# Loads, the V scratch and the opening of a fused attention and feed-forward kernel, rearranged

## The chip, the cores and the metric

The kernel runs on one core of a Trainium2 chip. The metric is the time of one execution on the device in microseconds (us), as the median of several runs. The engines are named as in the profile: PE (TensorE, matrix products), PEld (its loads of the stationary operand), DVE (VectorE), ACT (ScalarE), POOL (GpSimd) and SP (SyncE, which here only issues DMA transfers).

## The reference, cut to what matters

One transformer block is computed on 2048 tokens of width 512, in bfloat16. A modulation vector made from `c` and `w_mod` gives six rows of 512: shift, scale and gate of the attention (`sa`, `ca`, `ga`) and of the feed-forward part (`sb`, `cb`, `gb`).

```python
mod = (silu(c) @ w_mod).reshape(1, 6, 1, 512)
sa, ca, ga, sb, cb, gb = (mod[:, i] for i in range(6))
h = layernorm(x) * (1 + ca) + sa
q, k, v = split(h @ wqkv)                  # 32 heads of 16
idx = pos[:, None] - 2 * arange(8)         # each token sees 8 keys, 0, 2, .. 14 back
logits = einsum('hsd,hswd->hsw', q, k[idx]) * 16 ** -0.5   # -1e9 where idx < 0
x = x + ga * (einsum('hsw,hswd->hsd', softmax(logits), v[idx]) @ wo)
h = layernorm(x) * (1 + cb) + sb
x = x + gb * ((gelu(h @ w_gate) * (h @ w_up)) @ w_down)    # inner width 1792
```

## The kernel before

The tokens are worked on in four groups of 512, numbered 0 to 3 (`sg`). For each group the steps are these.

- `ln1`: mean and variance on DVE (L404, L405), the inverse root on POOL (L413), the normalized rows `xn` on DVE (L419).
- `t1`: the rows are transposed to `hT`. Group 0 does it on PE (L432) and scales while it leaves PSUM (L460 on DVE, L463 on ACT); the other groups use a transposing DMA issued by SP (L439) and scale in place on ACT (L447).
- `qkv`: twelve products of four matmuls each (L491), in the order q0, k0, v0 to v3, q1, k1, q2, k2, q3, k3; ACT copies each from PSUM (L506 q, L508 k, L512 v).
- `vload`: V of the group is stored to a scratch `vscr` in device memory (L518) and read back four times (L527), one read for each of four shifts, each into 32 of the 128 partitions of the tile `V`, so that the partitions hold V at the distances 0, 2, 4 and 6.
- `logits`, `soft`, `pv`: products of q and shifted k on DVE (L541), summed over the head on PE (L555), softmax, probabilities transposed on PE (L640), products with `V` on DVE (L658), summed on PE (L670).
- `x1`: product with `wo` (L690), added to x on DVE (L699); then `ln2`, another transposing DMA (`h` from `xn`, L439) and scaling on ACT (L447).
- `ffn`: 14 pairs of products with `w_gate` and `w_up` (L718), gelu and copy on ACT (L742, L749), their product on DVE (L760), 8 half products with `w_down` (L731), the residual on DVE (L767), and the store.

The program text doesn't fix the order of these steps. Each step is an `Op` of a thread; the threads have priorities from the table `PR` (lower goes first), one value for each kind of step and group. `Planner.run` takes the step that can begin first by its own model of engine times (`w`), buffers (`take`, `give`) and events (`after`, `fire`); among the steps of that engine that can begin within a tolerance (`slack`, or `far` for steps whose priority is better by 8 or more) it takes the one with the best priority. That order is then the program of each engine, and each engine executes its program strictly in order.

All loads but three are issued by SP, in the order of `sp_q`: x of group 0 in four pieces, the q and k blocks of `wqkv`, x of group 1, the v block of `wqkv`, x of groups 2 and 3, block 2 of `w_mod` (the row `ga`), four pieces of `wo`, blocks 3 and 4 of `w_mod` (for `mod1`, the second layer norm), block 5 (the row `gb`, by which `w_down` is scaled), then `w_gate` and `w_up` once V of group 0 has been read back, and `w_down` at the end. ACT issues `c` and the blocks 1 and 0 of `w_mod`, which the first layer norm needs (`mod0`). Until the first product PE runs 16 matmuls on zeros (`warmup`, L248).

`wqkv` lies in one tile `[128, DT, 3 * D]`: the three blocks are side by side inside each of the four slices `dt` over which a product sums. The scratch `vscr` is one tensor over all groups with rows of 2048 + 16.

## Time and profile before

| what | us |
|---|---|
| median of 3 runs | 254.66 (254.41 to 255.35) |
| profiled execution, its own time | 255.11 |
| its span, first to last instruction | 253.2 |
| PE busy / DVE busy / ACT busy / POOL busy | 240.3 / 185.2 / 144.6 / 15.3 |
| first product of `qkv` starts (L491) | 13.27 |
| first product of `ffn` of group 0 starts (L718) | 78.47 |
| last product ends | 249.7 |

The profile covers one execution. A busy PE is not PE at its peak: a single matmul of 128x512 shows 379 ns, but a row of them is started every 216 ns (56 matmuls of L731 take 12.10 us), and with the clock granted at one half every 0.43 us. `x8` in the timeline means eight instructions merged into one row, and the text in brackets is the time the engine had been idle before and what ended it. In the chain of waits a DMA row is the time from issue to landing.

### The profile page before, as it was taken

The page shows a single profiled execution, that of the slowest core. Times are in us where ns is not written, and L with a number is a line of the kernel's source. Part 1 is how long each engine was busy: PE and PEld are TensorE (multiplying, and loading weights), DVE is VectorE, ACT ScalarE, POOL GpSimd, SP SyncE. Part 2 cuts the span into 40 slices and gives each one's busy share as a digit, 9 for nine tenths or more (in the row PEclk, how much of TensorE's full clock was granted, in tenths as well). Part 3 has the DMA queues.
Part 4 walks back from the last instruction along what each step waited for, and adds up shares of the span by engine and source line. Part 5 has one row for each costly group of instructions (what it writes and reads, how often), then busy time and mean ns, then how long its engine had stood idle before and what let it go on. Part 6 is the DMA issues. An engine that isn't in the chain of part 4 may idle for free.

```text
span 253.2 us, 3608 instructions
## 1 busy us (share of the span) xinstructions
PE 240.3 (95%) x1353; PEld 105.2 (42%) x1353; DVE 185.2 (73%) x295; ACT 144.6 (57%) x237; POOL 15.3 (6%) x37
## 2 busy tenths in 40 slices
PE   6789698899999999999999999999999999999994
PEld 2444334434443433444444334444344444444441
DVE  3499949999999999999999969688948422222221
ACT  2065459978569967430796763448654730766400
POOL 3410003000200000002000001000001000000000
PEclk9799979999999999999999999999999999999999
DMA  6999899999983500973300069510000401000011
GB/s 213 350 332 283 166 193 188 356 346 255 198 190 116 183 0 0 203 137 71 81 16 1 0 129 197 116 43 23 0 0 3 84 21 52 11 4 0 0 41 41
DMA packets 37417, 29.41 MB, mean 116 GB/s; under 512 B 15512, under 2 KB 36248, under 8 KB 37400
## 3 DMA queue, kind: packets, MB, share of 16 engines
q1 hardware_dynamic: 36336, 28.14, 47.2%
q10 hardware_dynamic: 1064, 1.05, 1.3%
q8 instruction: 10, 0.16, 0.3%
q14 instruction: 7, 0.06, 0.1%
HBM read 21.32 MB, written 4.19 MB: 101 GB/s over the span
## 4 chain that ended last, share of the span: by engine, by line
PE 71%; DMA 14%; DVE 7%; ACT 5%; SPq 1%; issue 1%; DVEq 0%; ACTq 0%
PE y_ps L731 19%; PE g_ps L718 19%; PE u_ps L718 19%; DMA wm<-in_w_mod_dram 5%; PE x_ps L690 5%; PE qkv_ps L491 4%; PE o_ps L670 3%; DMA x<-in_A_x_dram 3%; DMA hT<-xn 3%; DMA h<-xn 2%; DVE st L404 2%; DVE pq L541 2%; ACT hT L447 1%; PE LTp L555 1%; ACT h L447 1%; DVE xn L419 1%
## 5 line engine op out<-in xcount | busy, mean ns | idle before, releaser
L718 PE MATMUL g_ps<-h,Wg 128*128 128x512 bf16 x224 | 57.9, 379 | 0.6 <-ACT h L447 0.3
L718 PE MATMUL u_ps<-h,Wu 128*128 128x512 bf16 x224 | 57.6, 379 | 0.0
L491 PE MATMUL qkv_ps<-hT,wqkv 128*128 128x512 bf16 x192 | 47.3, 390 | 3.9 <-ACT hT L447 2.6
L731 PE MATMUL y_ps<-WdP,hht 128*128 128x512 bf16 x224 | 49.3, 379 | 0.0
L742 ACT ACTIVATE gl<-g_ps 128x512 bf16<-128x512 f32 x56 | 33.5, 599 | 26.7 <-PE g_ps L718 23.3
L749 ACT CAST ub<-u_ps 128x512 bf16<-128x512 f32 x56 | 33.0, 588 | 20.2 <-PE u_ps L718 20.2
L760 DVE TENSOR_TENSOR hht<-gl,ub 128x512 bf16<-128x512 bf16 x56 | 23.5, 420 | 28.1 <-ACT ub L749 27.5
L658 DVE TENSOR_TENSOR pv<-PT,V 128x2048 bf16<-128x2048 bf16 x32 | 37.8, 1219 | 1.0 <-ACT PT L646 1.0
L541 DVE TENSOR_TENSOR pq<-qT,kT 128x2048 bf16<-128x2048 bf16 x32 | 37.8, 1216 | 0.4 <-ACT kT L508 0.4
L718 PEld LDWEIGHTS <-Wg 128*128 128x128 bf16 x224 | 21.1, 98 | 28.5 <-issue 4.6
L731 PEld LDWEIGHTS <-hht 128*128 128x128 bf16 x224 | 21.8, 98 | 26.4 <-issue 0.4
L718 PEld LDWEIGHTS <-Wu 128*128 128x128 bf16 x224 | 21.1, 98 | 27.7 <-issue 4.0
L491 PEld LDWEIGHTS <-wqkv 128*128 128x128 bf16 x192 | 20.9, 115 | 26.5 <-issue 9.8
L404 DVE BATCH_NORM_STATS2 st<-x 128x6 f32<-128x512 bf16 x32 | 21.7, 680 | 6.4 <-DMA x<-in_A_x_dram 6.3
L767 DVE TENSOR_TENSOR ot<-y_ps,x 128x512 bf16<-128x512 f32 x16 | 11.0, 687 | 21.1 <-PE y_ps L731 21.1
L413 POOL TENSOR_TENSOR rstd<-rstd,neghalf 128x4 f32<-128x4 f32 x8 | 10.7, 1340 | 178.9 <-DVE rstd L409 178.9
L447 ACT ACTIVATE h<-h,modT,scl 128x512 bf16<-128x512 bf16 x16 | 11.7, 803 | 7.1 <-DMA h<-xn 7.0
L690 PE MATMUL x_ps<-woP,oT 128*128 128x512 bf16 x64 | 15.6, 379 | 0.0
L508 ACT CAST kT<-qkv_ps 128x512 bf16<-128x512 f32 x16 | 9.2, 586 | 5.8 <-PE qkv_ps L491 5.8
L419 DVE TENSOR_SCALAR xn<-x,mv,rstd 128x512 bf16<-128x512 bf16 x32 | 11.4, 408 | 1.6 <-POOL rstd L413 1.5
L512 ACT CAST vT<-qkv_ps 128x512 bf16<-128x512 f32 x16 | 9.4, 588 | 5.2 <-PE qkv_ps L491 5.1
L699 DVE TENSOR_TENSOR x<-x_ps,x 128x512 bf16<-128x512 f32 x16 | 10.8, 683 | 1.7 <-PE x_ps L690 1.5
(62 smaller groups left out, 157.7 us busy)
## 6 DMA issues: line engine op xcount, KB each, us to landing
V<-vscr SPq DMA_DIRECT2D x12, 520.0 KB, 9.7
wm<-in_w_mod_dram SPq DMA_DIRECT2D x4, 512.0 KB, 9.8
vscr<-vT SPq DMA_DIRECT2D x4, 512.0 KB, 7.1
out_dram<-ot SPq DMA_DIRECT2D x16, 128.0 KB, 1.7
Wg<-in_B_w_gate_dram SPq DMA_DIRECT2D x1, 1792.0 KB, 7.5
Wu<-in_B_w_up_dram SPq DMA_DIRECT2D x1, 1792.0 KB, 11.9
WdP<-in_B_w_down_dram SPq DMA_DIRECT2D x1, 1792.0 KB, 7.5
wqkv<-in_A_wqkv_dram SPq DMA_DIRECT2D x3, 512.0 KB, 7.4
```

The costliest lines, as they stand in the source:

```text
L404: nc.vector.bn_stats(out=st_k["st"][:, c4, :], in_=src()[:, c4, :])
L419: nc.vector.tensor_scalar(out=B[key][:, c4, :], in0=src()[:, c4, :], scalar1=st_k["mv"][:, c4, 0:1], scalar2=st_k["rstd"][:, c4:c4 + 1], o ...
L447: nc.scalar.activation(out=h, in_=h, func=ACT.Identity, scale=sc(dt), bias=bi(dt))
L491: nc.tensor.matmul(ps[:].rearrange("p (c k) -> p c k", k=P), lhsT=wqkv[:, dt, blk * D + j:(blk + 1) * D:4], rhs=B["hT", sg][:, :, dt, :], ...
L541: nc.vector.tensor_tensor(out=pq[:], in0=_ap(B["qT", sg][:, j, :], [[0, 4], [1, SG]]), in1=_ap(kT[:, j, k0:k0 + SG], [[2, 4], [1, SG]]), o ...
L658: nc.vector.tensor_tensor(out=t[:], in0=_ap(B["PT", sg][:, wg, :], [[0, 4], [1, SG]]), in1=B["V4", sg][:, :, j, c0:c0 + SG], op=ALU.mult)
L690: nc.tensor.matmul(ps[:], lhsT=B["oT", sg][:, j, c4 * P:(c4 + 1) * P], rhs=woP[:, j, :], start=(j == 0), stop=(j == 3))
L718: nc.tensor.matmul(ps[:].rearrange("p (c k) -> p c k", k=P), lhsT=Wt[:, dt, ft * P:(ft + 1) * P], rhs=B["h2T", sg][:, :, dt, :], start=(dt ...
L731: nc.tensor.matmul(ps[:], lhsT=B["hh", sg, ft][:, c4 * P:(c4 + 1) * P], rhs=B["WdP"][:, ft, :], start=(ft == 0), stop=(ft == FT - 1))
L742: nc.scalar.activation(out=gl[:], in_=B["g", sg, ft][:], func=ACT.Gelu_apprx_tanh)
L749: nc.scalar.copy(out=ub[:], in_=B["u", sg, ft][:])
L760: nc.vector.tensor_tensor(out=hh[:], in0=B["gl", sg, ft][:], in1=B["ub", sg, ft][:], op=ALU.mult)
```

## The change

- `wqkv` becomes a tile `[128, 3, DT, D]`, each block on its own.
- The loads are cut into threads. `q_head` issues, all from SP: x of group 0 in two pieces (128 and 384 rows), blocks 1 and 0 of `w_mod`, q and k blocks, x of group 1, v block, x of group 2. Block 2 of `w_mod`, `wo` and x of group 3 may be issued only after the transposing DMA of group 1 has been; blocks 3, 4, 5, `w_gate` and `w_up` only after the reads of V of group 0 have been issued (and `w_gate` after the transposing DMA of group 2).
- The scratch is one tensor per group with rows of 512 + 16. The 16 positions before a group (the halo) are written into the tile `vT` by POOL (zeros for group 0, a copy of the end of the group before for the others). Each of the four reads takes, for each of 32 partitions, one contiguous run of 16 rows of 528, shifted by 0, 2, 4 or 6 elements, with `max_dma_last_dim=4 * VL`. The memsets of `V` on POOL go.
- The opening: the zeros for the warm-up come from DVE; the inverse root of group 0 is computed for rows 0 to 255 and 256 to 511 separately; the transposes of group 0 run in two halves; ACT reads one of the two PSUM tiles and DVE the other (before, both read both); `hT` of group 0 is contiguous; three further warm-up matmuls may run after `mod0`'s products.
- The planner's model gets eight DMA lanes, a hold of SP by the transposing DMA, an event "issued" (`!`) beside "landed", and other tolerances; the table `PR` is new.

```diff
@@ -16,15 +16,15 @@
 NEG = -1.0e9
 
 PR = {
-    "ga": 28, "mb": 30.4, "gb": -2.8, "wds": 56.8, "wos": 73.9, "ln1": [33.1, 16.9, 32.7, 29.1], "t1": [-35.2,
-    55, 3.9, 6.5], "h1": [4.7, 2.3, 4.2, 1], "qkv": [15, 5.4, 30.8, 36], "qev": [40, 53.9, 9, 22.7], "v":
-    [14.4, 70, 13, 46.1], "pq": [7.4, 84.3, 109.8, 154.6], "lmm": [4.5, 21.5, -2.4, 5.1], "lev": [2.2, 19.8,
-    38.5, 5.6], "smm": [4.6, 25, 3, -0.9], "soft": [23, 19.5, 1.7, 8.3], "e": [64, 19.2, 103, 16], "ptp": [8,
-    7.1, -1.7, 4.8], "pt": [-10.8, 0.2, 10.5, 42.3], "pv": [2.4, 11.1, 71.1, 29.2], "pvmm": [35.5, 31.3, 3.8,
-    4.1], "pvev": [-14.5, 64.7, 32.1, 40], "x1mm": [18.6, 1.6, -24.2, -9.1], "x1": [-12.8, 1.5, -0.7, -2],
-    "ln2": [28.5, 36.7, 1.4, 68.5], "t2": [1.8, -14.8, 3.9, 0.1], "h2": [-1, 17.3, -2, 10.1], "ffn": [45.9,
-    18, 20.7, 56.2], "act": [30.1, -13.5, -2.2, 57.1], "hh": [-5.2, -5.3, 0, 14.6], "st": [150.1, 14.3, 34.2,
-    31.2],
+    "q_wo": 19, "q_x": 40.9, "q_mb": -18, "q_gu": 55.1, "q_gb": -2.9, "vh": [44.4, 26.2, 17.2, 8], "ga": 87.3,
+    "mb": 20.6, "gb": 46.7, "wds": 31.8, "wos": 60.7, "ln1": [-10.7, 9, 24.7, 45.5], "t1": [-5.1, 14, 28,
+    19.5], "h1": [75.6, 67.7, -7.2, 8.7], "qkv": [13, 45.1, 43.6, 18], "qev": [95.8, 82.9, 35.4, 21.7], "v":
+    [70.1, 13.2, 40, 68.2], "pq": [42.8, 53, 75, 125], "lmm": [41.9, 0.2, 23, 40], "lev": [-14.8, 25.2, 8.6,
+    3], "smm": [-5.5, 13.4, 4.2, 31.5], "soft": [-9.7, 67.5, -8.6, 16.8], "e": [1.6, 53, 28, 33], "ptp":
+    [18.1, 0.5, 23, 4.1], "pt": [69.4, -1.3, 75.9, 32.8], "pv": [3, 6.6, 70, 44.8], "pvmm": [-9.7, 48, 33.5,
+    2], "pvev": [4, 48.8, 13.4, -0.6], "x1mm": [-2.1, 23.9, -6.5, -5.8], "x1": [-11.9, -1.2, -1.9, 23], "ln2":
+    [6, 56.2, 1.4, 23.4], "t2": [11.4, 40, 125.6, 7.2], "h2": [-6.5, -7.1, -11.7, 3], "ffn": [73.6, 51.6,
+    22.1, 81.7], "act": [40, -0.2, 18, 21.3], "hh": [-49, -19.9, -2.8, 7.2], "st": [1.4, 3.2, 13.1, 32.5],
 }
...
-        self.slack = {"PE": 0.51, "ACT": 0.68, "DVE": 0.14, "POOL": 0, "SP": 0}
-        self.far = {"PE": 0, "ACT": 0.05, "DVE": 0.21, "POOL": 0, "SP": 0}
+        self.slack = {"PE": 0.63, "ACT": 0.21, "DVE": 20.96, "POOL": 0, "SP": 84.59}
+        self.far = {"PE": 0, "ACT": 0.22, "DVE": 0.2, "POOL": 0, "SP": 10.66}
         self.table = None
         self.quad = False
         self.dma = 0.0
+        self.lanes = [0.0] * 8
...
             if op.dma:
                 self.dma = max(self.dma, t) + (op.lat or 0.0)
-                fin = max(end, self.dma) + self.LAT["SP"]
+                if op.hold:
+                    end = self.clock[eng] = max(end, self.dma)
+                fin = max(end if not op.hold else 0.0, self.dma) + self.LAT["SP"]
+                self.lanes = self.lanes[1:] + [fin]
             else:
                 fin = end + self.LAT[eng]
             for s in op.give:
                 s.free.append(fin)
             if op.fire:
                 self.done[op.fire] = fin
+                self.done[op.fire + "!"] = end
...
-    vscr = dram.tile([P, 4, VR], BF16, name="vscr")
+    vscr = [dram.tile([P, 4, VL], BF16, name=f"vscr{g}") for g in range(NSG)]
...
-    wqkv = pools["wA"].tile([P, DT, 3 * D], BF16, name="wqkv", tag="wA")
+    wqkv = pools["wA"].tile([P, 3, DT, D], BF16, name="wqkv", tag="wA")
...
-            B["V4", 0] = T("v4", [P, 4, 4, SG + 8], BF16, "V4")
-            for w4 in range(4):
-                nc.gpsimd.memset(B["V4", 0][H * w4:H * w4 + H, :, :, 0:8 + 2 * w4].rearrange("p i j s -> p (i j) s"), 0.0)
-        yield Op("POOL", 3.0, f2, take=[SL["v4"]], fire="M2", after=["LN1.0.rs"])
-
-    def warmup():
-        for k in range(16):
+        yield Op("POOL", 1.9, f2, fire="M2", after=["LN1.0.rs2"])
+
+    def warmup(n, zero):
+        if zero:
+            yield Op("DVE", 0.25, lambda: nc.vector.memset(gB[:], 0.0), fire="warm")
+        for k in range(n):
             def f(k=k):
                 if k == 0:
                     B["warm"] = T("mm", [P, SG], F32, "warm_ps")
-                nc.tensor.matmul(B["warm"][:], lhsT=ident[:], rhs=gB[:], start=True, stop=True)
-            yield Op("PE", 0.43, f, after=["warm"], take=[SL["mm"]] if k == 0 else [],
-                     give=[SL["mm"]] if k == 15 else [])
-
+                nc.tensor.matmul(B["warm"][:], lhsT=gB[:, 0:P], rhs=gB[:], start=True, stop=True)
+            yield Op("PE", 0.43, f, after=["warm"] if zero else ["warm", "mp0"], take=[SL["mm"]] if k == 0 else [],
+                     give=[SL["mm"]] if k == n - 1 else [])
+
+    ORDER = (0, 1, 2, 3)
...
-                (nc.scalar if b < 2 else nc.sync).dma_start(
+                nc.sync.dma_start(
...
-            return ld(wqkv[:, :, b * D:(b + 1) * D], wq_v[:, :, b * D:(b + 1) * D])
+            return ld(wqkv[:, b, :, :], wq_v[:, :, b * D:(b + 1) * D])
...
-            yield Op("ACT", 0.55, ldwm(1), take=[SL[WM[1]]], fire="wm1", lat=mb(0.5), dma=True)
-            yield Op("ACT", 0.55, ldwm(0), take=[SL[WM[0]]], fire="wm0", lat=mb(0.5), dma=True)
-
-        def sp_q():
-            for k in range(CPS):
-                yield Op("SP", 0.5, ldx(0, k, k + 1), fire=f"x0.{k}", lat=mb(0.125))
-            yield Op("SP", 0.55, ldq(0), fire="wqkv0", lat=mb(0.5))
-            yield Op("SP", 0.55, ldq(1), fire="wqkv1", lat=mb(0.5))
-            yield Op("SP", 0.55, ldx(1), fire="x1", lat=mb(0.5))
-            yield Op("SP", 0.55, ldq(2), fire="wqkv2", lat=mb(0.5))
-            yield Op("SP", 0.55, ldx(2), fire="x2", lat=mb(0.5))
-            yield Op("SP", 0.55, ldx(3), fire="x3", lat=mb(0.5))
-            yield Op("SP", 0.55, ldwm(2), take=[SL[WM[2]]], fire="wm2", lat=mb(0.5))
+
+        def q_head():
+            yield Op("SP", 0.45, ldx(0, 0, 1), fire="x0.0", lat=mb(0.125))
+            yield Op("SP", 0.45, ldx(0, 1, 4), fire="x0.1", lat=mb(0.375))
+            yield Op("SP", 0.5, ldwm(1), take=[SL[WM[1]]], fire="wm1", lat=mb(0.5))
+            yield Op("SP", 0.5, ldwm(0), take=[SL[WM[0]]], fire="wm0", lat=mb(0.5))
+            yield Op("SP", 0.5, ldq(0), fire="wqkv0", lat=mb(0.5))
+            yield Op("SP", 0.5, ldq(1), fire="wqkv1", lat=mb(0.5))
+            yield Op("SP", 0.5, ldx(1), fire="x1", lat=mb(0.5))
+            yield Op("SP", 0.5, ldq(2), fire="wqkv2", lat=mb(0.5))
+            yield Op("SP", 0.5, ldx(ORDER[2]), fire=f"x{ORDER[2]}", lat=mb(0.5))
+
+        def q_wo():
+            yield Op("SP", 0.5, ldwm(2), take=[SL[WM[2]]], fire="wm2", lat=mb(0.5), after=["LN1.1.t!"])
             for i in range(4):
-                yield Op("SP", 0.55, ld(woP[H * i:H * i + H, :, :], wo_v[i]), fire=f"wo{i}", lat=mb(0.125))
-            yield Op("SP", 0.65, ldwm(3), take=[SL[WM[3]]], fire="wm3", lat=mb(0.5))
+                yield Op("SP", 0.5, ld(woP[H * i:H * i + H, :, :], wo_v[i]), fire=f"wo{i}", lat=mb(0.125))
+
+        def q_x():
+            yield Op("SP", 0.5, ldx(ORDER[3]), fire=f"x{ORDER[3]}", lat=mb(0.5), after=["LN1.1.t!"])
+
+        def q_mb():
+            yield Op("SP", 0.65, ldwm(3), take=[SL[WM[3]]], fire="wm3", lat=mb(0.5), after=["V4ld.0!"])
             yield Op("SP", 0.65, ldwm(4), take=[SL[WM[4]]], fire="wm4", lat=mb(0.5))
-            yield Op("SP", 0.65, ldwm(5), take=[SL[WM[5]]], fire="wm5", lat=mb(0.5))
-            yield Op("SP", 0.65, ld(Wg[:], wg_v), fire="Wg", lat=mb(1.8), after=["V4ld.0"])
+
+        def q_gu():
+            yield Op("SP", 0.65, ld(Wg[:], wg_v), fire="Wg", lat=mb(1.8), after=["V4ld.0!", f"LN1.{ORDER[2]}.t!"])
             yield Op("SP", 0.65, ld(Wu[:], wu_v), fire="Wu", lat=mb(1.8))
+
+        def q_gb():
+            yield Op("SP", 0.65, ldwm(5), take=[SL[WM[5]]], fire="wm5", lat=mb(0.5), after=["V4ld.0!", "wm2!"])
+
+        def q_d():
             yield Op("SP", 0.65, ldwd, fire="Wd", lat=mb(1.8), take=[SL["wA"]], after=[f"qkv.{g}.l" for g in range(NSG)])
...
-        yield Op("SP", 2.3, f, after=[f"{ev}.x3"], take=[SL[dtag]], give=[SL["xn"]], fire=f"{ev}.t", lat=2.0)
+        yield Op("SP", 1.8, f, after=[f"{ev}.x3"], take=[SL[dtag]], give=[SL["xn"]], fire=f"{ev}.t", lat=1.9, hold=True)
...
+        for dd in range(2):
+            for dtp in range(2):
                 dt = 2 * dtp + dd
 
                 def f(dt=dt, dtp=dtp, dd=dd):
                     if dt == 0:
-                        B[dkey] = T(dtag, [P, CPS, DT, P], BF16, dtag)
-                    hp, h = B[key, dtp][:, dd, :].rearrange("p (c k) -> p c k", k=P), B[dkey][:, :, dt, :]
-                    if dve_share and dd == 1:
-                        nc.vector.tensor_scalar(out=h, in0=hp, scalar1=sc(dt), scalar2=bi(dt),
-                                                op0=ALU.mult, op1=ALU.add)
+                        B[dkey] = T(dtag, [P, DT, SG], BF16, dtag)
+                    hp, h = B[key, dtp][:, dd, :], B[dkey][:, dt, :]
+                    if dtp:
+                        nc.vector.tensor_scalar(out=h, in0=hp, scalar1=sc(dt), scalar2=bi(dt), op0=ALU.mult, op1=ALU.add)
                     else:
-                        nc.scalar.activation(out=h, in_=hp, func=ACT.Identity,
-                                             scale=sc(dt), bias=bi(dt))
-                onv = dve_share and dd == 1
-                yield Op("DVE" if onv else "ACT", 0.54 if onv else 0.68, f, after=[f"{ev}.t{dtp}"] + dep,
+                        nc.scalar.activation(out=h, in_=hp, func=ACT.Identity, scale=sc(dt), bias=bi(dt))
+                yield Op("DVE" if dtp else "ACT", 0.61 if dtp else 0.70, f, after=[f"{ev}.t{dtp}"] + dep,
                          take=[SL[dtag]] if dt == 0 else [], give=[SL["tp"]] if dd == 1 else [], fire=f"{ev}.h{dt}")
...
+        yield from norm(("xn1", sg), lambda: B["x", sg], lambda c4: [f"x0.{min(c4, 1)}"] if sg == 0 else [f"x{sg}"], ev,
+                        ((0, 2), (2, 4)) if sg == 0 else ((0, 4),))
+        pl.done[ev] = pl.done[f"{ev}.x3"]
...
+                        B["vT", sg] = T("vs", [P, 4, VL], BF16, "vT")
+                    nc.scalar.copy(out=B["vT", sg][:, j, VH:VL], in_=ps[:])
             yield Op("ACT", 0.53, g, after=[f"qp.{sg}.{blk}.{j}"], give=[SL["mm"]], fire=f"qkv.{sg}.{blk}.{j}")
...
+    def vhalo(sg):
+        def f():
+            if sg == 0:
+                nc.gpsimd.memset(B["vT", 0][:, :, 0:VH], 0.0)
+            else:
+                nc.gpsimd.tensor_copy(out=B["vT", sg][:, :, 0:VH], in_=B["vT", sg - 1][:, :, SG:VL])
+        yield Op("POOL", 0.4, f, after=[f"qkv.{sg}.2.3"] + ([f"vst.{sg - 1}"] if sg else []), give=[SL["vs"]] if sg else [],
+                 fire=f"vh.{sg}")
+
     def vload(sg):
         def f():
-            nc.sync.dma_start(out=vscr[:, :, VH + sg * SG:VH + (sg + 1) * SG], in_=B["vT", sg][:])
-        yield Op("SP", 0.65, f, after=[f"qkv.{sg}.2.3"], give=[SL["vs"]], fire=f"vst.{sg}", lat=1.5)
+            nc.sync.dma_start(out=vscr[sg][:], in_=B["vT", sg][:])
+        yield Op("SP", 0.65, f, after=[f"vh.{sg}"], give=[SL["vs"]] if sg == NSG - 1 else [], fire=f"vst.{sg}", lat=1.5)
         for w4 in range(4):
             def f(w4=w4):
-                if w4 == 0 and sg:
-                    B["V4", sg] = T("v4", [P, 4, 4, SG + 8], BF16, "V4")
-                z = 0 if sg else 8 + 2 * w4
-                src = bass.AP(vscr.tensor, vscr.offset + VH + sg * SG - 8 - 2 * w4 + z,
-                              [[16 * VR, H], [VR, 16], [1, SG + 8 - z]])
-                nc.sync.dma_start(
-                    out=B["V4", sg][H * w4:H * w4 + H, :, :, z:SG + 8].rearrange("p i j s -> p (i j) s"), in_=src)
-            yield Op("SP", 0.65, f, after=[f"vst.{sg}", "M2"], take=[SL["v4"]] if w4 == 0 and sg else [],
-                     fire=f"V4.{sg}.{w4}" if w4 < 3 else f"V4ld.{sg}", lat=2.8)
+                if w4 == 0:
+                    B["V4", sg] = T("v4", [P, 4 * 4, VL], BF16, "V4")
+                t, n = B["V4", sg], 4 * 4 * VL
+                d = t[H * w4:H * w4 + H, :, :].rearrange("p r s -> p (r s)")
+                src = bass.AP(vscr[sg].tensor, vscr[sg].offset, [[n, H], [1, n - 2 * w4]])
+                nc.sync.dma_start(out=d[:, 2 * w4:n], in_=src, max_dma_last_dim=4 * VL)
+            yield Op("SP", 0.65, f, after=[f"vst.{sg}"], take=[SL["v4"]] if w4 == 0 else [],
+                     fire=f"V4.{sg}.{w4}" if w4 < 3 else f"V4ld.{sg}", lat=1.7)
...
-                    c0 = 8 - 8 * wg
+                    c0 = VH - 8 * wg
                     nc.vector.tensor_tensor(out=t[:], in0=_ap(B["PT", sg][:, wg, :], [[0, 4], [1, SG]]),
-                                            in1=B["V4", sg][:, :, j, c0:c0 + SG], op=ALU.mult)
+                                            in1=B["V4", sg][:, j:16:4, c0:c0 + SG], op=ALU.mult)
...
+    pl.spawn(0.2, mods())
+    pl.spawn(0.5, warmup(16, True))
+    pl.spawn(30, warmup(3, False))
```

## Prediction

> **What bounds the kernel now.** I read first the page's 40 slices (6.33 us each), for the engine that sets the end.
>
> ```profile
> PE   6789698899999999999999999999999999999994
> DVE  3499949999999999999999969688948422222221
> PEclk9799979999999999999999999999999999999999
> DMA  6999899999983500973300069510000401000011
> ```
>
> From about 84 us on PE is full and at full clock to the end: what the change saves there it can only save by starting earlier. The gaps lie in the first 84 us, where DMA is full too (11 slices) and DVE nearly. So I asked the timeline of PE for that stretch.
>
> ```profile
> 13.27 0.38 PE L491 MATMUL qkv_ps<-hT,wqkv 128*128 128x512 bf16 x1 [0.48 <-ACT hT L463]
> 14.19 5.99 PE L491 MATMUL qkv_ps<-hT,wqkv 128*128 128x512 bf16 x27 [0.54 <-DMA wqkv<-in_A_wqkv_dram]
> ...
> 27.55 0.61 PE L555 MATMUL LTp<-pq,Mph 128*32 128x512 bf16 x8
> 29.82 0.38 PE L491 MATMUL qkv_ps<-hT,wqkv 128*128 128x512 bf16 x1 [1.66 <-ACT hT L447]
> ...
> 32.24 0.72 PE L555 MATMUL LTp<-pq,Mph 128*32 128x512 bf16 x8
> 32.90 3.44 PE L491 MATMUL qkv_ps<-hT,wqkv 128*128 128x512 bf16 x8
> ...
> 43.54 1.04 PE L338 MATMUL mb_ps<-wm,scT 128*128 128x512 bf16 x4 [0.72 <-DMA wm<-in_w_mod_dram]
> ```
>
> The second matmul of all waits for `wqkv`; the first product of group 1 waits for `hT`, and then eight matmuls take 3.3 us instead of 1.7. The granted clock by stretch (columns: length, then PE, PEld, DVE, ACT, POOL busy, clock, DMA share, GB/s) says why:
>
> ```profile
> 28.00:32.00 4.00, 1.36 (x8) 0.45 (x4) 3.90 (x8) 3.04 (x5) 0.94 (x1) 1.00 0.95 188
> 32.00:36.00 4.00, 4.00 (x17) 1.31 (x17) 1.39 (x5) 2.53 (x7) 0.07 (x1) 0.58 1.12 196
> ```
>
> PE was busy for 1.36 of 4 us, and in the next 4 us it got 0.58 of its clock. What made `hT` late is in the chain of waits (start, length):
>
> ```profile
> 4.18 8.37 DMA x<-in_A_x_dram
> ...
> 17.92 2.35 DVE pq L541 x2
> 20.26 1.29 DVE xn L419 x4
> 21.59 7.35 DMA hT<-xn
> 28.96 0.82 ACT hT L447
> 29.88 13.61 DMA wm<-in_w_mod_dram
> ```
>
> Two products `pq` stand before the normalized rows on DVE; the transposing DMA takes 7.35 us, where the three undisturbed ones for `h` take 4.3, because `wo` and three blocks of `w_mod` are queued ahead of it; block 5 of `w_mod` lands 13.6 us after its issue, behind the reads of V.
>
> **A ledger of PE** from 13.27 to 249.72, 236.45 us. Work at full clock: 936 matmuls of 128x512 at 0.216 = 202.2; 256 quarter-array ones at 0.55 per eight = 17.6; 64 transposes at 0.45 per eight = 3.6; 32 of `modT` 0.9; 32 changes back from quarter arrays at 0.11 (0.97 against 0.86 for four matmuls) = 3.5. Together 227.8, so 8.7 are lost: 0.7 at 13.27; 4.7 between 27.55 and 36.17 (8.62 less two eights, twelve matmuls and two changes); 0.7 at 43.5; 0.6 before `PTp` at 46.9; 1.1 where `ffn` of group 0 begins (78.47 to 83.64); 0.9 in crumbs. The change can win these 8.7 at most and what comes off the 13.27 before them.
>
> **Part by part.**
>
> *Opening.* x of group 0 and blocks 1 and 0 of `w_mod` are the same 1.6 MB that landed by 8.4; now x goes first. Its first piece landed at 3.0; the other 0.39 MB at 348 GB/s (the mean of 8 to 18 us) take 1.1 more, so some 5.1 instead of 7.8. Then: statistics of the second row block (0.69 + 0.18) and addition 0.17 to 6.2, POOL 1.0; meanwhile two more statistics to 7.9, addition to 8.1, POOL to 9.1, two `xn` at 0.35 to 9.9, eight transposes 0.7 to 10.7, ACT 0.77 twice: slice 0 at 11.6, slice 1 at 12.4; DVE's two (0.54) end before. `mod0` comes at 9.3 as before and is not last. So products start at 11.7. The wait for `wqkv` at 14.19 is a false one: the q block had landed at 9.55, but the second slice of q lies inside the span of the v block's write in the common tile, and that load landed at 14.1 (6.17 + 7.9). With separate blocks the q and k products (eight matmuls) run before v lands; v itself lands no earlier, since the same 3.7 MB are ahead of it. At 14.2 eight matmuls are done instead of one: 7 x 0.216 = **-1.5**. Bounds: -2.5 (PE as early as `hT`, with v early) to +0.8 (one queue starts slower than two: up to 4 us both moved little, 55 to 274 GB/s by half microseconds).
>
> *Group 1.* With priority 9 against 42.8 the normalization now precedes `pq`: x at 12.6, four statistics 3.5, addition and POOL 1.4, four `xn` 1.4, so 18.9; `wo`, block 2 and x of group 3 wait behind the DMA, so I take 4.3 for it: 23.2 instead of 28.9. ACT's four scalings (0.73) end at 26.2 instead of 31.9. PE ends group 0's products at 23.3 (14.2 + 40 x 0.216 + one eight); until 26.3 it has four matmuls (0.9) and one eight (0.5): 1.6 lost, and no half clock, since the hole is shorter. With some crumbs, 2.0 lost instead of 4.7: **-2.7**; bounds -4.5 to 0 (DMA as late as before).
>
> [...]
>
> *Block 5.* The row `gb` goes from priority -2.8 to 46.7, so its product stands behind other work: **-0.7**. But blocks 3, 4 and 5 are all issued after the reads of V now, and PE's order is fixed: if the planner puts a product too early, `qkv` queued behind it waits, as here for 0.7. Bounds -0.7 to +1.0.
>
> *V.* Sixteen reads and the halo: nothing waited for V (the `pv` products waited only for `PT`, 1.0 us), so longer runs bring **0**; the halo copies are POOL work (0.3 each by its memset row of 0.28) on an engine that is busy for 15 us of 253. Whether the reads get faster matters only for what queues behind them. The nearest rows, from the DMA view, at 30 to 40 us (V with 1 KB packets and block 5) and 46 to 49 us (`Wg`, 3.6 KB packets):
>
> ```profile
> DMA packets 1963, 1.93 MB, mean 193 GB/s; under 512 B 64, under 2 KB 1963, under 8 KB 1963
> DMA packets 342, 1.23 MB, mean 409 GB/s; under 512 B 0, under 2 KB 0, under 8 KB 342
> ```
>
> Between 2.8 and 1.3 us for a read of 0.54 MB; I take 2.8, because other 1 KB packets pass at 348, so size alone is not what halves the rate. [...]
>
> *`ffn` of group 0 and the rest.* Its start hangs on DVE's chain (pq, softmax, pv, x, second norm), which is full from 10 to 80 us but for 3.3 us at 32 to 36. New priorities reorder it in ways I can't read off; **0**, bounds -1.0 (the 1.1 there vanish) to +3.0 (PE has used up its `qkv` stock 3 us early and stands). Three more warm-up matmuls: 0, covered by the hole before `hT` (before, six of them ran from 8.83); 1.3 at half clock if they come later. Memset on DVE, one more addition: DVE idles until 3.0.
>
> Sum: -1.5 - 2.7 - 0.7 = -4.9. On the profiled execution 255.11 - 4.9 = 250.2; the median lies 0.45 lower, so **249.8**.
>
> **Rivals.**
>
> *A transposing DMA behind V (slower).* SP is one queue in order, and a transposing DMA holds it until what is ahead has passed: at 48.17 it held SP for 8.95 us and landed after 11.0, behind `Wg` and `Wu`. If that of group 2 is issued behind the store and the reads of V of group 0, these start at some 21 and take 1.5 + 4 x 2.8 to 34; it lands at 38 to 40, `hT` is ready at 41. Group 1's products end at 36.3: 5.5 us of hole less one eight, and 1.5 at half clock, +6.5 to +7: 249.8 + 7 = 256.8. It decides from 36 on, breaks even at 41. For it: the 8.95 row. Against it: priorities 28 for this DMA and 70.1 for V. Chance 0.14.
>
> *DVE sets the start of `ffn` (no change).* If its first product stays at 78.5, PE only reaches the same stock of work earlier and waits: 254.4. For it: DVE's 9s from slice 7 on. Against: 3.3 us of DVE's own hole also came from late `hT` and `LT`, and `pq` of later groups can be moved behind. Chance 0.11 (0.09 within 0.5%).
>
> *The reads don't do what they say.* Runs of 16,896, 16,892, 16,888 and 16,884 B with a cap of 2,112 B: if a run were cut into equal parts, 16,888 = 8 x 2,111 gives 67,552 parts of 8 B. The transposing DMA's packets (1,834 in 3 us on 16 engines) cost some 28 ns; 67,552 / 16 x 0.028 = 118 us for the third read of each group, over 700 us in all. Nothing in this trace shows how runs are cut. Chance 0.03, outside any useful range.
>
> **How the numbers follow.** Forecast 0.72, rivals 0.14, 0.11, 0.03. What this kernel's measurement can tell from no change is 0.5%, 1.27 us: faster is below 253.4, slower above 255.9. Faster 0.72 + 0.02 = 0.74, within 0.09, slower 0.14 + 0.03 = 0.17. The best bounds together, -2.5 - 4.5 - 0.7 - 1.0 = -8.7, give 246.0, the lower end; the upper end, 256.5, takes in the no-change case and most of the first rival, whose 256.8 and beyond, with the last, leave some 0.12 out.
>
> **What the changed profile would show.** Right: first L491 near 11.7, eight before a wait that ends with `wqkv` at about 14; DMA `hT<-xn` about 4.3 us, landing near 23; no stretch with clock under 0.9 after 14 us; no wait of `mb_ps` for DMA. Wrong: a product waiting for `hT` of group 2 or 3 with SP held over 5 us; a hole before the first L718; reads of V under 2 KB per packet by far.

## The result, and the profile after

The changed kernel takes 406.28 us (median; 401.20 to 413.30). The kernel before took 255.00 beside it, so the ratio is 1.572 (95% interval 1.555 to 1.589). The forecast was 249.8 with a range to 256.5: wrong in sign and size. The profiled execution took 413.3 us (span 411.4).

First the 40 slices of the page, now 10.3 us each (busy tenths, the granted clock, GB/s):

```profile
PE   6987400049980000699990019999400499999996
PEclk9899955558995555599997557999855599999999
DMA  8499999999999999802999970099999500030001
GB/s 263 147 226 186 19 14 14 12 322 343 112 11 11 11 11 121 272 0 62 57 14 14 14 142 14 1 109 14 14 14 54 99 13 1 2 76 25 2 13 38
```

PE was full and at full clock from 84 us on; now it stands four times. In each of those stretches the DMA engines are busy while 11 to 14 GB/s pass. The chain of waits and the packet count name the cause:

```profile
DMA packets 305289, 29.65 MB, mean 72 GB/s; under 512 B 290936, under 2 KB 302584, under 8 KB 305272
SPq 50%; PE 32%; DMA 10%; DVE 4%; ACT 3%; issue 1%; ACTq 0%; DVEq 0%
```

There are eight times the packets of before (37,417) for nearly the same bytes (29.41 MB), and half the chain is SP's queue: an issuing instruction that can't be issued. SP's timeline (start, length, instruction) shows which, and the page's list of issues (KB each, us to landing) which of the four reads it is:

```profile
34.43 47.16 SPq L560 DMA_DIRECT2D V<-vscr  x4
81.64 1.73 SPq L272 DMA_DIRECT2D wm<-in_w_mod_dram  x3
102.48 55.45 SPq L560 DMA_DIRECT2D V<-vscr  x4
158.47 6.55 SPq L462 DMA_TRANSPOSE h<-xn  x1
```

```profile
V<-vscr SPq DMA_DIRECT2D x4, 528.0 KB, 5.3
V<-vscr SPq DMA_DIRECT2D x4, 527.9 KB, 8.6
V<-vscr SPq DMA_DIRECT2D x4, 527.8 KB, 47.7
V<-vscr SPq DMA_DIRECT2D x4, 527.6 KB, 50.4
```

The third read, of 16,888 B per partition, takes 47.7 us, and the fourth, queued behind it, 50.4. The packet counts show how they were cut. In e2_nocap below, the same kernel without the cap, each run is one packet:

```profile
DMA packets 28169, 29.65 MB, mean 114 GB/s; under 512 B 15480, under 2 KB 25976, under 8 KB 27640
```

Against this row the changed kernel has 275,456 more packets under 512 B, 1,152 more from there to 2 KB, 1,024 more from 2 to 8 KB, and 512 fewer above. Each of the four reads has 4 x 32 = 128 runs (groups times partitions), so the four runs together became 2,152, 9 and 8 parts of these sizes. Exactly this comes out if the runs of 8,448, 8,446, 8,444 and 8,442 elements are cut into the fewest equal parts under the cap of 1,056 elements: 8 x 1,056, 41 x 206, 2,111 x 4 and 9 x 938, with 41 + 2,111 = 2,152. 8,444 = 4 x 2,111 with 2,111 prime, so the third falls into 2,111 parts of 4 elements, 8 B, for each of 32 partitions: 67,552 parts a read. SP stands at the fourth read for 45.5 us meanwhile, and everything behind it in its order is late. PE's timeline shows the first to suffer (the columns are start, busy time, engine, line, operation, and in brackets the idle time before and what ended it):

```profile
12.94 10.77 PE L515 MATMUL qkv_ps<-hT,wqkv 128*128 128x512 bf16 x47
26.66 1.04 PE L354 MATMUL mb_ps<-wm,scT 128*128 128x512 bf16 x4 [1.76 <-DMA wm<-in_w_mod_dram]
28.17 1.92 PE L515 MATMUL qkv_ps<-hT,wqkv 128*128 128x512 bf16 x8
88.31 0.58 PE L340 MATMUL modT_ps<-scT,wm 128*128 128x1 bf16 x16 [42.30 <-DMA wm<-in_w_mod_dram]
```

Blocks 3 and 4 of `w_mod` come behind the reads on SP; PE waits 42.3 us for them. Behind the reads of group 1 stands the transposing DMA for `h` (158.47 above), on which `ffn` of group 0 waits; it goes on so in groups 2 and 3.

### The profile page after: what moved, and what is told of

Its sections match the earlier page's. It is cut to its first block, busy times and chain, and to the rows that moved or that the text cites. A ratio compares the mean times of both kernels' runs of the same rounds, so it can differ in the third digit from the quotient of the medians.

```text
span 411.4 us, 3602 instructions
## 1 busy us (share of the span) xinstructions
PE 250.0 (61%) x1342; PEld 107.3 (26%) x1356; DVE 185.8 (45%) x297; ACT 145.8 (35%) x237; POOL 16.7 (4%) x37
## 4 chain that ended last, share of the span: by engine, by line
SPq 50%; PE 32%; DMA 10%; DVE 4%; ACT 3%; issue 1%; ACTq 0%; DVEq 0%
SPq L560 47%; PE u_ps L750 10%; PE g_ps L750 10%; PE y_ps L763 6%; DMA h<-xn 4%; DMA wm<-in_w_mod_dram 3%; PE qkv_ps L515 3%; DMA x<-in_A_x_dram 2%; ACT h L470 2%; PE o_ps L702 1%; SPq L462 1%; DVE pv L690 1%; DVE st L420 1%; DMA vscr<-vT 1%; PE x_ps L722 1%
## 5 line engine op out<-in xcount | busy, mean ns | idle before, releaser
L750 PE MATMUL g_ps<-h,Wg 128*128 128x512 bf16 x224 | 63.3, 399 | 77.6 <-ACT h L470 76.5
L750 PE MATMUL u_ps<-h,Wu 128*128 128x512 bf16 x224 | 60.2, 393 | 0.0
L470 ACT ACTIVATE h<-h,modT,scl 128x512 bf16<-128x512 bf16 x16 | 11.7, 801 | 122.2 <-DMA h<-xn 86.1
L515 PE MATMUL qkv_ps<-hT,wqkv 128*128 128x512 bf16 x191 | 46.4, 394 | 0.5 <-ACT vT L536 0.3
L653 DVE TENSOR_REDUCE mx<-e 128x128 f32<-128x1024 bf16 x4 | 7.5, 1877 | 49.5 <-ACT e L646 49.5
L340 PE MATMUL modT_ps<-scT,wm 128*128 128x1 bf16 x64 | 2.3, 165 | 44.5 <-DMA wm<-in_w_mod_dram 44.5
L587 PE MATMUL LTp<-pq,Mph 128*32 128x512 bf16 x128 | 10.5, 406 | 28.6 <-DVE pq L573 28.6
L430 POOL TENSOR_TENSOR rstd<-rstd,neghalf 128x4 f32<-128x4 f32 (+1 forms) x9 | 12.4, 1375 | 340.2 <-DVE rstd L426 340.2
L678 ACT COPY PT<-PTp 128x1024 bf16<-128x1024 bf16 x4 | 4.0, 1009 | 43.2 <-PE PTp L672 43.2
## 6 DMA issues: line engine op xcount, KB each, us to landing
V<-vscr SPq DMA_DIRECT2D x4, 527.8 KB, 47.7
V<-vscr SPq DMA_DIRECT2D x4, 527.6 KB, 50.4
```

The costliest lines, as they stand in the source:

```text
L470: nc.scalar.activation(out=h, in_=h, func=ACT.Identity, scale=sc(dt), bias=bi(dt))
L515: nc.tensor.matmul(ps[:].rearrange("p (c k) -> p c k", k=P), lhsT=wqkv[:, blk, dt, j:D:4], rhs=hview(B["hT", sg], dt), start=(dt == 0), st ...
L750: nc.tensor.matmul(ps[:].rearrange("p (c k) -> p c k", k=P), lhsT=Wt[:, dt, ft * P:(ft + 1) * P], rhs=hview(B["h2T", sg], dt), start=(dt = ...
```

## The experiments

Two questions were open: is it the cut alone, and what would the rest of the change have done? Line numbers differ by up to 34 between the kernels; the names of the tiles tell what is meant. Each ratio is against the kernel before on the same chip, where it took 255.0 to 255.7 us; medians from different chips can be compared no closer than that.

### How the runs are cut: four kernels

**e1_equal**: all four reads the same length, which divides well.

```diff
-  src = bass.AP(vscr[sg].tensor, vscr[sg].offset, [[n, H], [1, n - 2 * w4]])
-  nc.sync.dma_start(out=d[:, 2 * w4:n], in_=src, max_dma_last_dim=4 * VL)
+  src = bass.AP(vscr[sg].tensor, vscr[sg].offset + 8 - 2 * w4, [[n, H], [1, n - 8]])
+  nc.sync.dma_start(out=d[:, 8:n], in_=src, max_dma_last_dim=4 * VL)
```

> The changed kernel, but all four reads of V take runs of the same length, 8,440 elements, from position 8 of the tile on (the eight positions before are read by nobody), so that the same cap of 2,112 B divides them into 8 parts of 2,110 B; the programs of the four computing engines stay as they are. Theory 'cut' (the third read of each group went out in 2,111 parts of 8 B for each partition, held the DMA engines and SP some 45 us, four times): about 251 us (248 to 254), packets down from 305,289 to some 30,000, no SP row of V above 1 us. Rival 'order' (new priorities and late loads cost by themselves, the reads only part of it): above 260 us. Rival 'odd start' (what is slow is a destination that starts 4 to 12 B into the row): also about 251 here, so the run with parts of 16 B has to tell it apart.

Measured: 261.49 us, ratio 1.0225 (1.0184 to 1.0267). The cut's cost is gone, but the time is not the 251 of its theory: what is left is followed up below, by the rival *order* (new priorities and late loads cost by themselves).

**e2_nocap**: the change without its cap, one run of 16.9 KB per partition.

```diff
-  nc.sync.dma_start(out=d[:, 2 * w4:n], in_=src, max_dma_last_dim=4 * VL)
+  nc.sync.dma_start(out=d[:, 2 * w4:n], in_=src)
```

> The changed kernel without max_dma_last_dim: one run of 16,884 to 16,896 B for each partition, destination starting at 0, 4, 8 and 12 B. [...] Rival 'odd start': the third read stays near 45 us and the time near 400 us.

Measured: 259.94, ratio 1.0163 (1.0105 to 1.0221). The destinations start at 0, 4, 8 and 12 B here too, and the third read lands in 10.1 us, so the rival *odd start* is out.

**e3_rows**: rows of 1,040 B as in the kernel before, from the new scratch (these lines stand in place of the same two).

```diff
+  src = bass.AP(vscr[sg].tensor, vscr[sg].offset + 8 - 2 * w4, [[n, H], [VL, 16], [1, SG + 8]])
+  nc.sync.dma_start(out=t[H * w4:H * w4 + H, :, 8:VL], in_=src)
```

> The changed kernel with the reads of V in rows of 520 elements (1,040 B, 16 for each partition) as before the change, from the new scratch with halos. Theory 'cut': within 1.5 us of the run with equal parts, reads some 2.8 us each; so contiguous runs are worth nothing in the end time. Rival 'long runs help': slower than the equal parts by 2 us or more, because the transposing DMAs behind the reads come later.

Measured: 260.97, ratio 1.0197 (1.0163 to 1.0231).

**e4_cap16**: e1_equal with only the third read cut small, into 1,055 parts of 16 B: half the parts, the same bytes. Its second line becomes

```diff
+  nc.sync.dma_start(out=d[:, 8:n], in_=src, max_dma_last_dim=16 if w4 == 2 else 4 * VL)
```

> The run with equal lengths, but the third read of every group is capped at 16 B: 1,055 parts of 16 B for each partition instead of 2,111 of 8 B. Theory 'cut', price per part (45 us for 67,552 parts, 10.8 ns x 16 engines): 22.7 us for each such read; of the 151 us that the change lost some 156 were in four reads of 45 us less what was covered, so about 45 to 70 us above the equal parts, 300 to 325 us. If the price is per byte or from an odd start and not per part: near 400 us, or near 251 us.

Measured: 323.01, ratio 1.2599 (1.2547 to 1.2652). The DMA view over a stretch that holds nothing but the cut read (48 to 78 us), of the changed kernel, and SP's timeline of e4_cap16:

```profile
DMA packets 51160, 0.41 MB, mean 14 GB/s; under 512 B 51160, under 2 KB 51160, under 8 KB 51160
```

```profile
34.51 27.41 SPq L560 DMA_DIRECT2D V<-vscr  x4
82.20 26.83 SPq L560 DMA_DIRECT2D V<-vscr  x4
141.94 27.96 SPq L560 DMA_DIRECT2D V<-vscr  x4
200.86 26.46 SPq L560 DMA_DIRECT2D V<-vscr  x4
```

51,160 parts in 30 us on 16 engines are 9.4 ns for each; e4_cap16's parts of 16 B run at 27 GB/s, 9.5 ns each. At these two sizes the price is per part, not per byte. The SP holds add up to 195.7 us in the changed kernel and 108.7 in e4_cap16, against 8.0 for the uncut reads of e2_nocap, and the times stand 146 and 63 us above e2_nocap: in both, some 10 us of each hold cost nothing. So **146 of the 151 us are the cut read**. And the long runs bring nothing: e1, e2 and e3 lie within 1.6 us, with overlapping intervals. The first and the last of the four reads in e2_nocap's list of issues:

```profile
V<-vscr SPq DMA_DIRECT2D x4, 528.0 KB, 5.7
V<-vscr SPq DMA_DIRECT2D x4, 527.6 KB, 12.0
```

With issues 0.5 us apart they land one each 2.6 us: 0.54 MB at 208 GB/s in runs of 16.9 KB. In runs of 1 KB it is 198 GB/s (e3_rows, the page's slice of 38.9 to 45.4 us).

All three kernels are still **slower** than before, by 4.3 to 5.8 us, where the forecast had -4.9. PE's timeline of e2_nocap, and its granted clock (the last columns of a window: clock, DMA share, GB/s):

```profile
28.64 1.04 PE L354 MATMUL mb_ps<-wm,scT 128*128 128x512 bf16 x4 [2.82 <-DMA wm<-in_w_mod_dram]
...
50.59 0.55 PE L340 MATMUL modT_ps<-scT,wm 128*128 128x1 bf16 x16 [3.38 <-DMA wm<-in_w_mod_dram]
51.01 0.61 PE L672 MATMUL PTp<-ident,e 128*128 128x128 bf16 x8
53.27 0.59 PE L340 MATMUL modT_ps<-scT,wm 128*128 128x1 bf16 x16 [1.66 <-DMA wm<-in_w_mod_dram]
53.72 5.92 PE L515 MATMUL qkv_ps<-hT,wqkv 128*128 128x512 bf16 x16
```

```profile
55.00:59.00 4.00, 4.00 (x12) 1.48 (x11) 1.20 (x2) 1.36 (x3) 0.00 (x0) 0.58 1.03 414
```

The products of blocks 2, 3 and 4 stand in PE's order where their weights have not landed: 7.9 us of waits in these three rows, and most of sixteen matmuls at half clock. A trace is one execution, here the slowest of four (261.84 us), and the opening scatters: the first product of `qkv` starts here at 14.09 us, in e5_mb_early below at 12.09, with the same order of loads up to there. So a trace tells where a loss lies, and the medians tell its size. A theory follows: the order of the loads costs the rest.

### The order of the loads: six kernels

In these the planner's list of steps is kept, and single loads are moved in it before the program is written, so that PE, DVE, ACT and POOL keep e2_nocap's order:

```diff
-            op.fn()
+            self.seq.append([op.fire or op.tag, op.fn])
...
+        move(["wm3", "wm4"], after="vst.0")
+        for e in seq:
+            e[1]()
```

**e5_mb_early** has the move shown.

> The kernel of e2_nocap with two loads moved in SP's order: the weights of the modulations' blocks 3 and 4 are issued right after group 0's write of V, ahead of the four reads back; the orders on PE, DVE, ACT and POOL are those of e2_nocap. Theory (what is lost beside the cut reads is lost by the load order: products on PE wait for weights that queue behind the reads): the waits of 3.38 and 1.66 us of the modT products near 50 us go, and with them most of the half clock of the 16 products after them (some 2.5 us); time about 252 to 253 against 259.94 of e2_nocap. Rival (PE's waits are only where another chain shows itself: DVE and ACT set the end of group 2): the waits move to another place and the time stays at 257 or more.

Measured: 255.86, ratio 1.0021 (1.0004 to 1.0039). 4.1 us less than e2_nocap (3.6 by the two ratios), of 7 to 8 expected. The two waits and the half clock behind them are gone, but `mb_ps` still waits 2.0 us for block 2, with half clock after it, and 1.6 us went to `PTp` and `o_ps`, which now wait for DVE.

**e6_mb_wo_early**

```diff
+        move(["wm2", "wo0", "wo1", "wo2", "wo3", "x3"], after="x2")
```

> The kernel of e5_mb_early, and besides it the weights of the modulations' block 2, the four of the output projection and the third group's rows issued right after the second group's rows, and not behind the first layer norm of group 1. Theory of the load order: the wait of 2.82 us for block 2's weights near 28 us goes too, and the DMA queues no longer stand idle from 14 to 20 us; time about 250, 2% under the kernel before. Rival: these loads now share the queues with the first weights of qkv, so that the first products wait longer, by up to 3 us, and the time is that of e5_mb_early or above it.

Measured: 255.30, ratio 0.9988 (0.9962 to 1.0013): no difference from before, where about 250 was expected. PE is 2 us ahead of the kernel before at 45 us (the same sixteen matmuls started at 47.32) and loses it again; its timeline, and the waits of DVE:

```profile
45.33 3.62 PE L517 MATMUL qkv_ps<-hT,wqkv 128*128 128x512 bf16 x16
50.70 0.40 PE L704 MATMUL o_ps<-pv,Msum 128*32 128x512 bf16 x4 [1.75 <-DVE pv L692]
51.84 0.44 PE L704 MATMUL o_ps<-pv,Msum 128*32 128x512 bf16 x4 [0.74 <-DVE pv L692]
52.22 3.50 PE L517 MATMUL qkv_ps<-hT,wqkv 128*128 128x512 bf16 x8
```

```profile
DVE pv L692 <- DMA V<-vscr: 2.9, 1, 2.9
```

Now V itself is late: its reads are issued at 31.2 us, because the store of V stands on SP behind group 2's transposing DMA, which is held to 27.1. What was nothing before ("nothing waited for V") has become the wait that ends last.

**e9_order**: the reads of V ahead of that transposing DMA.

```diff
+        move(["wm2", "wo0", "wo1", "wo2", "wo3", "wm3", "wm4", "x3"], after="x2")
+        move(["vst.0", "V4.0.0", "V4.0.1", "V4.0.2", "V4ld.0"], after="LN1.1.t")
```

> The kernel of e2_nocap with SP's order near that of the kernel before, the orders of the other engines as in e2_nocap: the weights of the modulations' blocks 2, 3 and 4, those of the output projection and the third group's rows follow the second group's rows, and group 0's write of V and its four reads back come right behind group 1's transposing DMA, ahead of group 2's. In e6_mb_wo_early PE stood 2.0 us ahead of the kernel before at 45 us (45.33 against 47.32 at the same 16 products) and lost it where DVE waited 2.9 us for V (1.75 and 0.74 us on PE, and 1.6 us of half clock). Theory (the order of the loads is all that was lost): V lands before DVE asks for it, the first FFN product starts near 76 to 77 us in place of 79.6, and the time is 251 to 253, about 1% under the kernel before. Rival (DVE's 8 products of 9.2 us and the sums behind them set the end of group 2 whatever the loads): the time is within 0.7 us of e6_mb_wo_early.

**e10_wo_late**: the same with `wo` behind the reads (`move(["wo0", ..., "wo3"], before="wm5")`).

> The kernel of e9_order with the four loads of the output projection's weights issued behind the four reads of V in place of ahead of group 1's transposing DMA: 2.8 us less of issuing on SP and 0.5 MB less on the queues in the opening. Theory: group 1's transposed rows and V come up to 1 us earlier and the time is 0 to 1 us under e9_order. Rival: the scaling of these weights on DVE, which stood at 38.8 us, waits for them, and the time is above e9_order by 1 us or more.

Measured: 265.94, ratio 1.0423 (1.0404 to 1.0442), and 262.65, ratio 1.0283 (1.0264 to 1.0302). Both theories of e9_order were wrong. SP's and PE's timelines of e9_order:

```profile
28.41 2.06 SPq L562 DMA_DIRECT2D V<-vscr  x4
30.58 10.76 SPq L464 DMA_TRANSPOSE hT<-xn  x1
```

```profile
47.08 1.03 PE L621 MATMUL LNp<-ident,LT 128*128 128x128 bf16 x8 [9.49 <-DVE LT L610]
```

The transposing DMA stands 10.8 us at the head of SP behind four reads. PE does not wait for its rows: ACT does (10.6 us, `hT` of group 2), in its order, and behind ACT's wait are the copies that release `LT`. e10_wo_late is 3.3 us better than e9_order, more than expected: group 1's transposing DMA is held 2.9 us in place of 6.1.

**e11_vst_first**: e10_wo_late with the reads behind that DMA again, and only V's store ahead of it (`move(["vst.0"], after="LN1.1.t")`).

> The kernel of e10_wo_late with group 2's transposing DMA ahead of the four reads of V again: behind group 1's transposing DMA come group 0's write of V, group 2's transposing DMA, the four reads and then the weights of the output projection; the orders of the other engines as in e2_nocap. In e9_order and e10_wo_late that DMA stood 10.8 and 10.5 us at the head of SP behind the reads, ACT, in its order, waited for the transposed rows in front of the copies that release LT, and PE stood 9.5 and 10.0 us at LNp. Theory (what cost there is the transposing DMA behind the reads, and the load order is what e2_nocap lost): no wait at LNp, V issued near 28 us in place of 31.2 in e6_mb_wo_early and landed before DVE asks for it at 46.5, first FFN product 76 to 78 us, time 251 to 253.5. Rival (DVE sets the end of group 2): within 0.7 us of e6_mb_wo_early, 254.6 to 256.

Measured: 257.47, ratio 1.0066 (1.0041 to 1.0091). The wait at `LNp` is gone, as expected, and V is in time; but `wo`, now behind the reads, is late, and the time is above what both sides expected. The waits of DVE, and PE's timeline behind it, where sixteen matmuls then take 6.05 us instead of 3.6 (this trace is the slowest of seven executions, 259.65 us):

```profile
DVE woP L406 <- DMA woP<-in_A_wo_dram: 4.3, 1, 4.3
```

```profile
50.04 1.03 PE L674 MATMUL PTp<-ident,e 128*128 128x128 bf16 x8 [5.55 <-DVE e L665]
51.34 6.05 PE L517 MATMUL qkv_ps<-hT,wqkv 128*128 128x512 bf16 x16
```

**e12_wm_wo_early**: e6_mb_wo_early with V's store ahead of the transposing DMA.

```diff
+        move(["wm2", "wo0", "wo1", "wo2", "wo3", "x3"], after="x2")
+        move(["vst.0"], after="LN1.1.t")
+        move(["wm3", "wm4"], before="V4.0.0")
```

> The kernel of e6_mb_wo_early with group 0's write of V ahead of group 2's transposing DMA instead of behind it; the weights of blocks 3 and 4 still ahead of the four reads. One step between e6_mb_wo_early and e11_vst_first. Theory: V's reads are issued about 2 us earlier than in e6_mb_wo_early (29 in place of 31.2), DVE's wait for V of 2.9 us shrinks to about 1, time about 254. Rival: the transposing DMA of group 2 is held by the write by as much as the write gains, its rows reach ACT later than LT's copies can spare, and the time is 256 or more.

Measured: **251.57, ratio 0.9851 (0.9827 to 0.9874)**, the one kernel that is faster than the kernel before, by 1.5%. Its clock row (a 9 is 90% or more), its waits on PE (total, times, longest), and the first product of `ffn`:

```profile
PEclk9999999999999999999999999999999999999999
```

```profile
PE modT_ps L342 <- DMA wm<-in_w_mod_dram: 1.7, 1, 1.7
PE warm_ps L252 <- DVE gB L247: 1.3, 1, 1.3
PE PTp L674 <- DVE e L665: 1.2, 1, 1.2
PE x_ps L724 <- DVE x L733: 1.0, 1, 1.0
PE LTp L589 <- DVE pq L575: 1.0, 2, 0.7
```

```profile
75.34 0.94 PE L752 MATMUL g_ps<-h,Wg 128*128 128x512 bf16 x3
```

V's reads are issued at 28.8 in place of 31.2 us; DVE's wait for V, the two waits of PE for `pv` and the half clock are all gone, some 2 us more than the theory gave. From the first `ffn` product to the end of the span 174.7 us pass. Before it was 253.2 - 78.47 = 174.7, in e2_nocap 260.0 - 85.89 = 174.1, and in all twelve profiled kernels without a read cut small it is 174.1 to 174.8. There the time is set by what stands before the first `ffn` product.

### The opening: two kernels

**e8_before_tile**: the kernel before, with `wqkv` laid out block by block and nothing else.

```diff
-    wqkv = pools["wA"].tile([P, DT, 3 * D], BF16, name="wqkv", tag="wA")
+    wqkv = pools["wA"].tile([P, 3, DT, D], BF16, name="wqkv", tag="wA")
...
```

> The kernel before with one edit of the change alone: the weights of qkv laid out block by block; every engine's order is that of the kernel before. By the prediction's first step: 1.5 us less than the kernel before (first product at 11.7 us in place of behind the last block's load). Rival: the transposed rows of group 1 come no earlier, so PE waits for them by what it gained, and the time is the same within 0.4 us.

Measured: 255.34, ratio 1.0001 (0.9985 to 1.0016): nothing. PE's timeline of it:

```profile
13.34 0.38 PE L491 MATMUL qkv_ps<-hT,wqkv 128*128 128x512 bf16 x1 [0.49 <-ACT hT L463]
14.21 6.01 PE L491 MATMUL qkv_ps<-hT,wqkv 128*128 128x512 bf16 x27 [0.50 <-DVE hT L460]
```

Against the rows of before (13.27; 14.19, 0.54 for `wqkv`), the false wait is gone and the second matmul starts no earlier: now it waits for DVE's slices of `hT` (L460). In the profile of before DVE began them at 13.40, two in 1.07 us, so that the first was ready near 13.9 and only some 0.3 us could be had; here DVE begins at 13.64, behind x, and even that is gone. Neither theory had this reason, though the rival had the time.

**e7_tile**: e2_nocap with the common tile of before (the same edit backwards).

> The kernel of e2_nocap with the weights of qkv in one common tile laid out as in the kernel before, so that the three blocks' loads and products share one tile; every engine's order is that of e2_nocap. By the prediction's first step the first product waits for the load of the whole tile's latest block, near 14 us in place of near 13, and the time is 1.0 to 1.5 us above e2_nocap. Rival: what opens earlier is swallowed by the next wait (the weights of block 2 near 28 us), and the time is within 0.5 us of e2_nocap.

Measured: 260.27, ratio 1.0193 (1.0169 to 1.0217), not to be told from e2_nocap. In this opening the false wait is real (second matmul at 14.45 us, 1.12 for `wqkv`), and the time doesn't show it. That the later waits for `w_mod` swallow it is likely, but not shown: the opening scatters by more.

## Why the prediction was wrong

**The step that failed first** is the part *V*, which put the sixteen reads at 0, and the rival *The reads don't do what they say*, which had the mechanism to the last digit (16,888 = 8 x 2,111, 67,552 parts of 8 B) and a chance of 0.03. "Nothing in this trace shows how runs are cut" was a reason for a large chance, not for a small one: of two ways to cut, equal parts or cap-sized parts with a rest, one costs 150 us. Its price was also off, by a factor of 3 per part (28 ns from a transposing DMA's packets; 9.4 measured), and a fifth of each hold cost nothing: 146 us in all, where four times 118 were said.

**The step that failed second** is *Block 5*, bounds -0.7 to +1.0. It saw that blocks 3, 4 and 5 were now issued after the reads of V, and that a product put too early would hold `qkv`; but it took the 0.7 us of the one such wait of before as the price. Measured: 3.4 and 1.7 us of waiting for blocks 3 and 4 and a stretch at half clock, some 4 us in all by e5_mb_early. Block 2, deferred in the change behind group 1's transposing DMA, was not in the sum at all (1.8 us in the changed kernel, 2.8 in e2_nocap). Block 5 itself came in time.

*Opening*, -1.5: the new layout of `wqkv` by itself **0** (e8_before_tile). The wait put down to `wqkv` was only the last of two, and DVE's slice ended some 0.3 us before it. With the rest of the opening, eight products did run ahead of the v block, as said, but the block landed later than the 14.2 of the sum, as the loads of PE's weights in the changed kernel show:

```profile
14.88 8.35 PEld L515 LDWEIGHTS <-wqkv 128*128 128x128 bf16 x40 [0.53 <-DMA wqkv<-in_A_wqkv_dram]
```

The 48 products of group 0 end at 23.55 there, against 25.10 before less 0.55 for the eight `LTp` among them: 1.0 us won in that execution. In the eleven profiled kernels with this opening they end between 22.91 and 25.11, at the median at 24.12, so that some 0.4 of the 1.5 us are left. The first product came at 12.94 in place of 11.7, behind 16 products for `modT` that waited 1.8 us for their weights and four warm-up matmuls at half clock, which the sum had at 0. In that sum, x at 5.1 us should have been 4.1 by its own terms (3.0 + 1.1); 4.4 was measured. The bound in which one queue starts slower than two is not borne out: up to 4 us 0.60 MB passed in the changed kernel, 0.49 MB in the one before.

*Group 1*, -2.7: right in its mechanism. The transposing DMA took 4.4 us (4.3 said), the rows came at 24.2 (23.2 said) and the eight matmuls ran in 1.92 us at full clock. That a hole of 3.0 us with 1.4 us of work in it brings no half clock was an estimate, and no run shows how long a hole may be: here the granted clock was 1.00 from 14 to 40 us, in e5_mb_early 0.57 behind a hole of 2.05 us. But `LNp` behind them started at 36.9, later than the 36.2 of before: block 2 cost 1.8 us, and ACT stood 2.7 us for group 2's transposing DMA (5.1 us on SP, behind block 2, `wo` and x), with the copies for `LT` behind that wait. The gain shows only where these loads are early too: `LNp` starts at 34.4 in e12_wm_wo_early, so -1.8 with the opening, where -4.2 were said.

The rival *A transposing DMA behind V* didn't happen in the changed kernel, whose order has group 2's ahead of the reads. But it is real, and its hole was set too short: 5.5 us said, 9.5 and 10.0 on PE in e9_order and e10_wo_late. In time it is 10.6 us between e6_mb_wo_early and e9_order, which differ also in the place of blocks 3 and 4, and 5.2 between e10_wo_late and e11_vst_first, where `wo` is waited for next; 6.5 to 7 were said.

*`ffn` start*: that the time is decided before 78 us held in every kernel without the cut; the 4.9 us were nearly there to be had (4.0 by e12_wm_wo_early), with a load order that the change doesn't have. The rival that DVE holds this start at 78.5 us is out: it came at 75.34 there. What of the gain comes from the reordered work of the other engines and what from the halos stays open: the kernel before with SP's new order, or e12_wm_wo_early with the old scratch, wasn't run.

## What to carry to other kernels

A cap on the length of a DMA run cut it here into equal parts, whatever their size (8,444 elements under a cap of 1,056 into 2,111 parts of 4): before trusting one, factor the run length, and give runs a length with a divisor just below the cap (8,440 = 8 x 1,055 in e1_equal), or no cap. A load that is issued later to make room for another must be followed to the instruction that consumes it on every in-order engine: here block 2, blocks 3 and 4, V and `wo` became in turn the wait that ended last, as the one before it was mended. A wait that the trace puts down to one cause is worth removing only if no second one ends just before it; the timeline of the producers around that moment tells.

## What the runs showed of the hardware

- A part of 8 B and one of 16 B cost the same, 9.4 and 9.5 ns on each of 16 engines; a read of 0.54 MB in 8 B parts fell from 208 to 14 GB/s.
- The next issue on the same engine was held meanwhile: that of the fourth read held SP for 45.5 us.
- Reads into 32 partitions pass at some 200 GB/s with runs of 1 KB (198 in e3_rows) and of 16.9 KB (208 in e2_nocap) alike.
- Half clock came in e6_mb_wo_early after holes of 1.75 and 0.74 us, with four quarter-array matmuls between them (a window at 0.57), and in e5_mb_early after one of 2.05 (0.57 too). Length alone doesn't decide: after a hole of 2.82 us in e2_nocap four matmuls took 1.04 us, at full clock. What does decide isn't shown here. The windows after the holes, of e6_mb_wo_early and e5_mb_early:

```profile
52.00:56.00 4.00, 4.00 (x20) 1.15 (x16) 3.19 (x3) 1.42 (x3) 0.00 (x0) 0.57 1.04 419
26.00:30.00 4.00, 3.59 (x15) 0.93 (x16) 3.66 (x4) 1.62 (x3) 0.00 (x0) 0.57 1.11 230
```
